# Another written order for the first two batches of an attention and expert kernel, with the loads placed anew

## The chip, the core and the metric

The kernel runs on one core of a Trainium2 chip. What counts is the time of one execution on the device in microseconds. Five engines work beside each other, each through its own list of instructions in order: TensorE (PE, with its weight loads as PEld), VectorE (DVE), ScalarE (ACT), GpSimd (POOL) and SyncE (SP), which here only issues the loads and stores. An instruction waits on semaphores for what it reads and for the buffer that it writes.

## What is computed

Attention in two steps with 32 packed queries, and then a layer of three products with a maximum:

```python
def sm_attn(qq, kk, vv):                       # head_dim 64
    s = scale * np.matmul(qq, kk.transpose(0, 1, 3, 2))
    s = s - np.max(s, axis=-1, keepdims=True)
    a = np.exp(s)
    a = a / (np.sum(a, axis=-1, keepdims=True) + 1e-09)
    return np.matmul(a, vv)
p_packed = sm_attn(p, k, v)                    # 8 batches, 8 heads, 32 x 64
out = sm_attn(q, p_packed, p_packed)           # 8 batches, 8 heads, 576 x 64
...
x = out.transpose(0, 2, 1, 3).reshape(4608, 512)
h = np.maximum(np.maximum(x @ w1, x @ w2), x @ w3)   # 512 -> 768
return (h @ w_out).astype(np.float32)                # 768 -> 512
```

All in float32.

## The kernel before

The work goes batch by batch, eight of them, 576 tokens each. Since `out` is a product of weights and `p_packed`, the kernel never forms x: it multiplies `p_packed` by the weights once (stage P, 4 x 2 blocks of 32 rows in 64 contraction rows) and the second softmax by that. Each product of N and O is formed from a high and a low part in the fp32r type, three matmuls for one.

The stages have letters. k, v, q and w are loads; w0 to w5 are the six column tiles of w1, w2, w3, each in three parts of 512 KB (`w01` is tile 0, part 1), and w6 is w_out. S is the scores of the packed queries with k (L226); A weighs them: DVE's maximum (L239) and scaling (L240), ACT's exp (L244), and, in the first two batches, the turning T of the weights by PE (L269, L270) and a copy. Z inverts the sums. V is the product with v (L312), K turns p_packed (L327) and copies it to `pt`. Q is the scores of q with it (L341), in two halves of 288 tokens. B (`attend`) is the second softmax: DVE's block transpose (L364), maximum (L368), subtraction (L370), ACT's exp (L372), sum (L375), reciprocal (L382), product (L384), transpose (L387) and the split into a2h and a2l (L126 to L131). C converts one part of a weight: two steps on ACT (L189, L194), one on DVE (L200), one on POOL (L204). P is p_packed @ w for one tile (L414), which ACT and DVE then split into ph (L425) and pl (L427). N (`layer_in`, L450) multiplies a2 by P, E takes the maximum (L465), H splits it, O (`layer_out`, L504) is the product with w_out, F scales and stores. P04 is batch 0, tile 4. The filler matmuls of `rouse` (L139, on the identity) are placed by a word `I10`: ten units of 128 columns ahead of the next product.

What sets the order: the words of the table START are taken one after the other, and each advances its stage by one step, so the table is the order of every engine's list for batches 0 and 1 and the first parts of batch 2. A letter v, g or a behind a word (`B000g`) names the engine of a step where there is a choice: DVE, POOL or ACT. Loads stand in the same table, and they go to SP's one queue in that order. Behind the table, a loop over batches 2 to 7 starts each batch's stages at the times of STAGES, counted in steps of PE, and only PE's order is fixed by hand there; for the batch 2 the loop begins with two tiles of P.

PSUM is two buffers of two banks (`ps_big`) for S, Q, the pairs of P and the T of batch 1, and four buffers of one bank (`ps_moe`) for N, O and the single tiles of P. So with S1 in both large buffers, the next product that wants one, P01, waits for the first exp of S1 (it is the last to read it), and the one behind, T10, for the second. Loads of k and v share four buffers, those of q two, of weights seven and four.

Where PE stands at a time is told by the word and its number: Q0's first half is at 14.47 us, its second at 18.81, P00 at 20.30, S1 at 25.73 and 27.10, P01 at 30.79, T10 at 31.60, V1 at 35.24, Q1 at 38.52.

Of the kernel before, what the change touches and what calls it, by code (L numbers as in the profile page):

```python
# [44 lines left out]


START = """
k01 k00 w00 I10 S0 A01 v00 v01 w02 C00 A01 A00 A00 I7 A01 A01v A00 q000 q010 C00 w01 I1 V01 C00 C00 A00v
Z00 Z01 q011 C02 V01 V00 q001 V00 w21 K0 K0v C02 C01 I1 Q0 C02 B000 B000 B010 C01 C02 B010 B000g C01
B000 B010v w11 w10 B000 w12 I8 Q0 B000a B010 C21 B001 B000 C21 C01 I3 P00 B011 B000g B001 B001g P00 B011  # L50
B000 C21 B011v B000a B000g C21 B001 B011 B010 B001 B010a B011 B010 k10 k11 C10 B001a w20 P00 I10 N00
B011a B001 B011 B001v B010v w32 w22 C10 C11 C10 I4 S1 B011v B010 B001 C12 C11 B010a C10 B011 B010v C11
C12 P00 C12 P00 B001a C20 N00 A10 N00 B011a v11 v10 C20 C11 A11 C12 A10 w40 A11 P01 B001v q10 q11 E000v
B011g E000 Z11 P01 C32 C32 C20 Z10 C20 A10 N00 N00 P01 C32 A10v A11 N00 C22 A11a E001v C40 C22 E000 V101
E001 V101 C32 N01 w30 w31 K1 C22 w61 E001 C22 C40 K1a H00a N01 w62 Q1 C30 E010v C40 H00v B11 B10 C40 C30
H00v N01 C30 C30 C31 N01 E010 B10 P02 P02 E010 C31 P10 B10g E011v w42 P02 N01 w63 C31 N01 B11 C61 w41
C31 E011 w60 B10 C42 E011 N02 C42 N02 P03 H01a N02 C42 N02 B10 E020v C42 B10v E020 H01g P03 C41 E021a
N02 N02 B11g E020 P03 C41 E021 H01v C41 N03 N03 C41 P10 B10 P10 E021 H02v E030v C61 B11 B11 E030 N03 w52
w51 w50 P11 P04 B10g C61 B11v C52 C62 E030 N03 C62 P04 C50 H02g N03 P04 B11 C63 H02a E031a B10 E031 N03
B10a N04 N04 E040a B11g C51 N04 E031 B11 E040 B10v C51 C51 B11a N04 B11v C50 C52 E041a N04 N04 H03a C61  # L60
E040 E041 E041 N10 H03v C62 C50 C52 H03a E100v H04a P11 N10 N10 C50 E100 C51 P11 E100 N10 C63 E101a N10
N10 N11 E101 H04v H04a E110v N11 N11 E110 C52 P05 P12 E101 N11 N11 P05 C61a H10a P05 E111a C60 P12 C62
E110 N11 C61g H10v E111 N05 E111 H11v P12 C60 C62a H10a E050a N05 N05 E050 N05 N12 E051v H11g E050 C62v
N05 N05 P13 P14 E051 N12 H11v E051 C60 E120a P14 H05v C63 N12 w64 w65 P13 H05g E120 C63 C60 N12 N12 N12
P13 E121a C65 E120 H05v N13 C63v E121 E121 E130a H12a q21 k20 k21 C64 C60a C65 P14 C64 N13 N13 C63g H12g
C60g E130 N13 P15 E131a E130 C64 P15 N13 N13 H12a C65 P15 E131 C64 N14 N14 S2 C64v E131 N14 N14 C65
E140v A20 O0 A21 C65v E140 E140 C65g C64v A20 A21 v21 q20 k30 X2 v20 X2 N14 O0 O0 O0 k31 E141v N14 O0 X2
O0 F00v E141 E141 Z21 O0 O0 O0 F01a O0 O0 F02a O0 N15 H13a F03v H13v H13a N15 N15 V201 E150v Z20 V201
N15 K2 N15 E150 N15 K2v E151v E150 E151 Q2 O1 O1 O1 B21 E151 H15a O1 B20 B21 H14a B20 H14v H15g O1 v31
O1 O1 B20v B21g B21 B20 O1 B20 P20 F10a B21 B21a v30 O1 O1 F11a B20a B20 B20g q31 B20 O1 H15v B21 q30  # L70
B21g B20a P20 B21 P20 B20g B21a O1 B21v F13a H14a F12v
"""

EXTRA = "12 05 13"
# [3 lines left out]
STAGES = "S1:2 k2:5 X1:7 P3:12 P4:12 P5:25 V1:25 K1:29 v2:28 Q1:36 P6:36 q2:38 P7:42 P8:42"  # L78
# [3 lines left out]
def fused_kernel(ctx: ExitStack, tc: tile.TileContext, kp, qt, va, vb, wi, wo, out):  # L82
# [483 lines left out]
    def begin(stage, at):  # L566
        due.append([at, len(due), stage])

    def tick():

        while True:
            ready = [d for d in due if d[2] is not None and d[0] <= clock[0]]
            if not ready:
                break
            d = min(ready, key=lambda d: d[:2])
            wait = next(d[2], None)
            while wait == 0:
# [14 lines left out]
    def issue(name, b, at):  # L592

        kind, n = name[0], int(name[1])
        if kind == "P":
            b, j = b + n // NJ, n % NJ
        else:
            b += n
        if b >= B:
            return  # L600
        if kind in loads:
            begin(both(loads[kind], b), at)
        elif kind == "P":
# [82 lines left out]
```

## Time and profile before

| | |
|---|---|
| median of three runs | 482.77 us (482.42 to 483.08) |
| profiled execution, its own time | 483.46 us |
| span of the profiled execution | 481.7 us |
| PE busy | 471.6 us (98% of the span) |
| DVE, ACT, POOL busy | 253.4, 191.2, 130.5 us |
| chain that ended last | PE 93%, DMA 5% |

The chain that ended last is the work followed back from the last instruction, at each step to what released it; it is PE's matmuls for 93% of the span. The span is cut into 40 slices of 12.04 us in the page, and a digit is the busy share in tenths.

### The profile page before, as it was taken

To read this page: it belongs to the slowest core of one execution; us is meant where nothing else is said; L and a number is where in the kernel's file an instruction comes from. 1 tells how busy PE (TensorE), PEld (TensorE's weight loads), DVE (VectorE), ACT (ScalarE), POOL (GpSimd) and SP (SyncE) were. 2 spreads that over 40 slices of the span, in tenths; PEclk is the share of its full clock that TensorE was granted. 3 is DMA by queue.
4 is the path that set the end of the run, shared out by engine and by line. 5 is a ranking of instruction groups with operands and counts; after the bars stand their busy time and mean duration, and the time that the engine had idled before them with its cause. 6 is when DMAs were issued, how large, how long until landed. Compare 5 with 4: busy or idle time off the path is not lost.

```text
span 481.7 us, 10570 instructions
## 1 busy us (share of the span) xinstructions
PE 471.6 (98%) x4352; PEld 388.6 (81%) x4352; DVE 253.4 (53%) x540; ACT 191.2 (40%) x409; POOL 130.5 (27%) x108
## 2 busy tenths in 40 slices
PE   7789999999999999999999999999999999999997
PEld 3367999888769987899679987899778987999885
DVE  2799988833656465444826455444816455244100
ACT  3687854401335334333424334333334334244211
POOL 0666754600322222022312223032212213144000
PEclk9999999999999999999999999999999999999999
DMA  8999221664245241423324242423221101100122
GB/s 298 398 378 405 97 81 72 216 177 148 69 169 144 60 151 49 156 44 99 105 84 138 51 136 79 152 51 101 98 88 25 27 2 45 44 1 1 44 67 65
DMA packets 36767, 55.60 MB, mean 115 GB/s; under 512 B 21488, under 2 KB 23792, under 8 KB 36720
## 3 DMA queue, kind: packets, MB, share of 16 engines
q1 hardware_dynamic: 36720, 54.93, 34.1%
q8 instruction: 34, 0.56, 0.5%
q14 instruction: 13, 0.11, 0.1%
HBM read 41.94 MB, written 9.44 MB: 107 GB/s over the span
## 4 chain that ended last, share of the span: by engine, by line
PE 93%; DMA 5%; ACT 0%; SPq 0%; issue 0%; DVE 0%; ACTq 0%
PE mi L450 48%; PE mo L504 32%; PE pw L414 7%; DMA wi<-in_wi 2%; PE av L312 2%; DMA q<-in_qt 2%; PE s L341 2%; DMA v<-in_va 2%; PE s L226 2%; PE tp L312 0%; PE tp L269 0%; SPq L160 0%; ACT wi L189 0%; PE av L327 0%; ACT a L244 0%
## 5 line engine op out<-in xcount | busy, mean ns | idle before, releaser
L450 PE MATMUL mi<-a2h,ph 128*128 128x288 f32 x576 | 173.6, 301 | 0.0
L450 PE MATMUL mi<-a2h,pl 128*128 128x288 f32 x576 | 169.8, 295 | 0.4 <-DVE pl L427 0.4
L450 PE MATMUL mi<-a2l,ph 128*128 128x288 f32 x576 | 169.7, 295 | 0.0
L465 DVE TENSOR_TENSOR hf<-mi,hf 128x288 f32<-128x288 f32 x192 | 86.5, 453 | 110.5 <-PE mi L450 87.5
L504 PE MATMUL mo<-h,wo_hi 128*128 128x512 f32 x432 | 139.5, 398 | 0.0
L450 PEld LDWEIGHTS mi<-a2h,ph 128*128 128x128 f32 x576 | 108.1, 188 | 13.5 <-issue 7.8
L450 PEld LDWEIGHTS mi<-a2h,pl 128*128 128x128 f32 x576 | 108.1, 188 | 1.0 <-DVE pl L427 0.7
L450 PEld LDWEIGHTS mi<-a2l,ph 128*128 128x128 f32 x576 | 108.1, 188 | 0.0
L131 POOL TENSOR_TENSOR h<-hf,h 128x512 fp32r<-128x512 f32 x36 | 46.5, 1292 | 220.0 <-ACT h L126 134.8
L504 PEld LDWEIGHTS mo<-h,wo_hi 128*128 128x128 f32 x432 | 81.0, 187 | 26.4 <-issue 4.2
L504 PE MATMUL mo<-h,wo_lo 128*128 128x512 f32 x216 | 85.3, 395 | 0.0
L427 DVE SCALAR_TENSOR_TENSOR pl<-pw,ph 128x768 fp32r<-128x768 f32 (+1 forms) x54 | 45.0, 860 | 34.7 <-ACT ph L425 34.5
L126 ACT COPY hf<-mi 128x288 f32<-128x288 f32 x83 | 33.0, 397 | 63.3 <-PE mi L450 58.2
L126 ACT CAST h<-hf 128x512 fp32r<-128x512 f32 x45 | 27.8, 620 | 60.4 <-DVE hf L465 60.4
L524 ACT ACTIVATE o<-mo 128x512 f32<-128x512 f32 x32 | 19.1, 597 | 77.7 <-PE mo L504 71.0
L504 PEld LDWEIGHTS mo<-h,wo_lo 128*128 128x128 f32 x216 | 40.5, 188 | 9.1
L425 ACT ACTIVATE ph<-pw 128x768 fp32r<-128x768 f32 (+1 forms) x54 | 37.9, 738 | 11.4 <-PE pw L414 10.8
L414 PE MATMUL pw<-w_sb,pt 64*32 64x384 f32 x768 | 38.2, 489 | 0.7 <-ACT a L244 0.7
L204 POOL TENSOR_TENSOR w_sb<-w_sb,wi 128x512 int32<-128x512 int32 x18 | 24.1, 1343 | 26.4 <-DVE w_sb L200 18.4
L370 POOL TENSOR_TENSOR e<-e,m 128x576 f32<-128x576 f32 (+1 forms) x15 | 16.7, 1127 | 29.8 <-DVE m L368 29.8
L131 POOL TENSOR_TENSOR a2l<-et,a2h 128x576 fp32r<-128x576 f32 (+1 forms) x13 | 17.5, 1348 | 21.0 <-ACT a2h L126 20.9
L414 PEld LDWEIGHTS pw<-w_sb,pt 64*32 64x32 f32 x768 | 11.4, 106 | 13.2 <-issue 11.4
(91 smaller groups left out, 339.4 us busy)
## 6 DMA issues: line engine op xcount, KB each, us to landing
kt<-in_kp SPq DMA_DIRECT2D x16, 640.0 KB, 5.2
wi<-in_wi SPq DMA_DIRECT2D x18, 512.0 KB, 8.2
out_t<-o SPq DMA_DIRECT2D x35, 256.0 KB, 2.0
v<-in_va SPq DMA_DIRECT2D x16, 512.0 KB, 4.6
q<-in_qt SPq DMA_DIRECT2D x14, 576.0 KB, 5.5
wo<-in_wo SPq DMA_DIRECT2D x6, 512.0 KB, 6.9
xt<-x SPq DMA_DIRECT2D x48, 40.0 KB, 2.0
xt<-x SPq DMA_DIRECT2D x48, 32.0 KB, 1.9
```

The lines of the kernel that those rows point to most:

```text
L126: e.copy(out=out, in_=src)
L131: on(default).tensor_tensor(out=lo, in0=src, in1=hi.bitcast(F32), op=ALU.subtract)
L204: nc.gpsimd.tensor_tensor(out=dst.bitcast(I32), in0=dst.bitcast(I32), in1=up, op=ALU.add)
L226: nc.tensor.matmul(out=s1[b][r][32 * n:32 * n + 32, hf, 0:HS], lhsT=kt[g][o, w:w + NP], rhs=kt[g][o, pr * S + hf * HS:pr * S + (hf + 1) * HS],
L370: on("g").tensor_tensor(out=e3, in0=e3, in1=m.unsqueeze(2).to_broadcast([P, nt, NP]), op=ALU.subtract)
L414: nc.tensor.matmul(out=ps[r][NP * n:NP * n + NP, 0:NW * P], lhsT=pt_sb[b % 2][o, NP * n:NP * n + NP], rhs=w_sb[o, j, n * NW * P:(n + 1) * ...
L425: nc.scalar.activation(out=hi[:, r], in_=x, func=AF.Copy, scale=2.0 ** -WS)
L427: nc.vector.scalar_tensor_tensor(out=lo[:, r], in0=x, scalar=2.0 ** -WS, in1=hi[:, r].bitcast(F32), op0=ALU.mult, op1=ALU.subtract,)
L450: nc.tensor.matmul(out=sums[b, j, hf, x][:, 0:HS], lhsT=w[:, r, x * P:(x + 1) * P], rhs=a[:, c], start=(r == 0 and n == 0), stop=(r == R - ...
L465: nc.vector.tensor_tensor(out=h, in0=sums[b, j, hf, i][:, 0:HS], in1=h, op=ALU.max)
L504: nc.tensor.matmul(out=sums[b, m], lhsT=w[:, j, m * P:(m + 1) * P], rhs=h[:, a], start=(j == 0 and i == 0), stop=(j == NJ - 1 and i == 2),)
L524: nc.scalar.activation(out=o, in_=ps, func=AF.Copy, scale=2.0 ** -WS)
```

## The change

The table START is written anew from end to end, with the same stages and steps, and the first tile of P of batch 2, `P1:0`, that the loop began with is now in it (as `P21`). Five single tiles and five pairs of P are in both. The fillers are 44 units before (10, 7, 1, 1, 8, 3, 10, 4) and 49 after (10, 7, 1, 1, 3, 27). A letter of choice differs at many words. The beginning of the table and the line of the loop:

```diff
-k01 k00 w00 I10 S0 A01 v00 v01 w02 C00 A01 A00 A00 I7 A01 A01v A00 q000 q010 C00 w01 I1 V01 C00 C00 A00v
+k01 k00 w02 v01 I10 S0 A01 C02 A01 v00 A00 Z01 A00 w12 I7 A01 A01v A00 A00v q000 C02 I1 V01 Z00 V01 C02
...
-            for x in (STAGES if b > 2 else "P1:0 P2:0 " + STAGES).split():
+            for x in (STAGES if b > 2 else "P2:0 " + STAGES).split():
```

On SP, the loads from the first weight behind v to k of batch 1 (kt2, kt3), before:

```order
L154 DMA wi0_2_119<-in_wi 128x512
L175 DMA q0_151<-in_qt 128x2x288
L175 DMA q1_153<-in_qt 128x2x288
L154 DMA wi0_1_156<-in_wi 128x512
L175 DMA q1_153<-in_qt 128x2x288
L175 DMA q0_151<-in_qt 128x2x288
L154 DMA wi2_1_218<-in_wi 128x512
L154 DMA wi1_1_249<-in_wi 128x512
L154 DMA wi1_0_251<-in_wi 128x512
L154 DMA wi1_2_255<-in_wi 128x512
L160 DMA kt2_315<-in_kp 128x1280
L160 DMA kt3_317<-in_kp 128x1280
```

and now:

```order
L154 DMA wi1_2_133<-in_wi 128x512
L175 DMA q0_157<-in_qt 128x2x288
L175 DMA q1_214<-in_qt 128x2x288 x2
L175 DMA q0_157<-in_qt 128x2x288
L154 DMA wi0_0_232<-in_wi 128x512
L154 DMA wi0_1_238<-in_wi 128x512
L154 DMA wi1_1_258<-in_wi 128x512
L154 DMA wi1_0_267<-in_wi 128x512
L160 DMA kt2_306<-in_kp 128x1280
L160 DMA kt3_308<-in_kp 128x1280
```

w00, which stood ahead of v, and w01 now come behind all four parts of q; w12 stands ahead of q, and w21 behind kt3. So the fourth part of q has one weight fewer in front of it, and kt3 too.

On PE, from N behind S1 to N behind T10 (S1 is s1_1, P01 is pw0_1), before:

```order
L450 MATMUL mi0_0_0_1_325<-a2h0_1_373,pl0_0_292 128x288
L450 MATMUL mi0_0_0_1_325<-a2l0_1_377,ph0_0_291 128x288
L450 MATMUL mi0_0_0_2_326<-a2h0_1_373,ph0_0_291 128x288
L450 MATMUL mi0_0_0_2_326<-a2h0_1_373,pl0_0_292 128x288
L450 MATMUL mi0_0_0_2_326<-a2l0_1_377,ph0_0_291 128x288
L414 MATMUL pw0_1_424<-w_sb_72,pt0_76 32x384 x8
L269 MATMUL tp1_0_455<-ident_67,a1_1_0_416 128x128 x4
L270 MATMUL tp1_0_455<-ident_67,a1_1_0_416 64x128
L450 MATMUL mi0_0_1_0_461<-a2h0_0_300,ph0_0_291 128x288
L450 MATMUL mi0_0_1_0_461<-a2h0_0_300,pl0_0_292 128x288
```

and now, from the end of S1:

```order
L226 MATMUL s1_1_0_334<-kt3_308 32x288
L226 MATMUL s1_1_1_335<-kt3_308 32x288
L450 MATMUL mi0_0_0_0_382<-a2h0_0_301,ph0_0_327 128x288
L450 MATMUL mi0_0_0_0_382<-a2h0_0_301,pl0_0_328 128x288
L450 MATMUL mi0_0_0_0_382<-a2l0_0_332,ph0_0_327 128x288
L450 MATMUL mi0_0_0_1_383<-a2h0_0_301,ph0_0_327 128x288
L450 MATMUL mi0_0_0_1_383<-a2h0_0_301,pl0_0_328 128x288
L450 MATMUL mi0_0_0_1_383<-a2l0_0_332,ph0_0_327 128x288
L414 MATMUL pw0_1_391<-w_sb_72,pt0_76 32x384 x8
L450 MATMUL mi0_0_0_2_384<-a2h0_0_301,ph0_0_327 128x288
L450 MATMUL mi0_0_0_2_384<-a2h0_0_301,pl0_0_328 128x288
L450 MATMUL mi0_0_0_2_384<-a2l0_0_332,ph0_0_327 128x288
```

Before, six N stood ahead of S1 and twelve between S1 and P01. Now P00 and S1 follow each other without N or filler, six N stand between S1 and P01, and N that stood ahead of P01 stand behind it.

On POOL, the conversions L204 and the steps of the second softmax of batch 0 between them, before:

```order
L204 TENSOR_TENSOR w_sb_72<-w_sb_72,wi0_1_156 128x512
L384 TENSOR_TENSOR e0_0_235<-e0_0_235,z2_0_0_0_253 128x288
L370 TENSOR_TENSOR e0_0_235<-e0_0_235,m2_0_0_288_288 128x288
L131 TENSOR_TENSOR a2l0_0_302<-et0_0_296,a2h0_0_300 128x288
L204 TENSOR_TENSOR w_sb_72<-w_sb_72,wi2_1_218 128x512
L204 TENSOR_TENSOR w_sb_72<-w_sb_72,wi1_0_251 128x512
L204 TENSOR_TENSOR w_sb_72<-w_sb_72,wi1_1_249 128x512
```

and now:

```order
L370 TENSOR_TENSOR e0_1_236<-e0_1_236,m2_0_1_0_253 128x288
L204 TENSOR_TENSOR w_sb_72<-w_sb_72,wi0_0_232 128x512
L384 TENSOR_TENSOR e0_0_228<-e0_0_228,z2_0_0_288_277 128x288
L204 TENSOR_TENSOR w_sb_72<-w_sb_72,wi0_1_238 128x512
L204 TENSOR_TENSOR w_sb_72<-w_sb_72,wi1_1_258 128x512
L204 TENSOR_TENSOR w_sb_72<-w_sb_72,wi1_0_267 128x512
L384 TENSOR_TENSOR e0_1_236<-e0_1_236,z2_0_1_288_295 128x288
```

w01 (wi0_1) stood first of these and now comes behind w00 and one L384; the L204 of w11 and w10 follow it directly.

On DVE, around the products L384 of that softmax, before:

```order
L382 RECIPROCAL z2_0_1_288_312<-z2_0_1_288_312 128x9
L384 TENSOR_TENSOR e0_0_235<-e0_0_235,z2_0_0_288_309 128x288
L384 TENSOR_TENSOR e0_1_239<-e0_1_239,z2_0_1_0_307 128x288
L200 TENSOR_SCALAR w_sb_72<-wi1_0_251 128x512
L384 TENSOR_TENSOR e0_1_239<-e0_1_239,z2_0_1_288_312 128x288
L387 STREAM_TRANSPOSE et0_1_368<-e0_1_239 128x288
L387 STREAM_TRANSPOSE et0_0_296<-e0_0_235 128x288
L387 STREAM_TRANSPOSE et0_1_368<-e0_1_239 128x288
L131 TENSOR_TENSOR a2l0_1_377<-et0_1_368,a2h0_1_373 128x288
```

and now:

```order
L382 RECIPROCAL z2_0_0_288_277<-z2_0_0_288_277 128x9
L384 TENSOR_TENSOR e0_0_228<-e0_0_228,z2_0_0_0_260 128x288
L370 TENSOR_TENSOR e0_1_236<-e0_1_236,m2_0_1_288_279 128x288
L200 TENSOR_SCALAR w_sb_72<-wi0_1_238 128x512
L382 RECIPROCAL z2_0_1_0_274<-z2_0_1_0_274 128x9
L384 TENSOR_TENSOR e0_1_236<-e0_1_236,z2_0_1_0_274 128x288
L375 TENSOR_REDUCE z2_0_1_288_295<-e0_1_236 128x9
L387 STREAM_TRANSPOSE et0_0_297<-e0_0_228 128x288
L387 STREAM_TRANSPOSE et0_1_303<-e0_1_236 128x288
L200 TENSOR_SCALAR w_sb_72<-wi1_0_267 128x512
```

The L200 of w01 now stands behind an L384 and an L370 and ahead of another L384; in the order before, w01's came far earlier, and w10's stands in this place.

## Rows read from the trace of the kernel before

**Rows 1.** The page's forty slices: PE's busy tenths and those of the transfers

```profile
PE   7789999999999999999999999999999999999997
...
DMA  8999221664245241423324242423221101100122
```

**Rows 2.** Windows: stretch, length, busy PE, PEld, DVE, ACT, POOL, clock, DMA share, GB/s

```profile
0.00:31.00 31.00, 24.47 (x257) 12.22 (x265) 19.37 (x56) 17.99 (x39) 13.53 (x18) 1.00 0.96 356
31.00:478.00 447.00, 447.00 (x4103) 376.43 (x4087) 233.61 (x483) 172.83 (x370) 116.92 (x91) 1.00 0.30 99
```

**Rows 3.** PE's waits for loads: engine, tile, releaser, total us, times, longest

```profile
PE s L341 <- DMA q<-in_qt: 1.6, 1, 1.6
PE s L226 <- DMA kt<-in_kp: 1.5, 2, 0.8
```

**Rows 4.** PE's timeline: start, duration, line, operation, count, and the idle time before

```profile
18.81 0.72 PE L341 MATMUL s<-q,pt 64*32 64x288 f32 x16 [1.61 <-DMA q<-in_qt]
...
20.30 0.88 PE L414 MATMUL pw<-w_sb,pt 64*32 64x384 f32 x16
21.11 2.42 PE L139 MATMUL mi<-ident 128*128 128x512 f32 x6
23.18 0.48 PE L450 MATMUL mi<-a2h,ph 128*128 128x288 f32 x1
...
27.10 1.18 PE L226 MATMUL s<-kt 64*32 64x288 f32 x24 [0.68 <-DMA kt<-in_kp]
...
28.45 0.29 PE L450 MATMUL mi<-a2h,pl 128*128 128x288 f32 x1
28.58 0.29 PE L450 MATMUL mi<-a2l,ph 128*128 128x288 f32 x1
...
30.79 0.88 PE L414 MATMUL pw<-w_sb,pt 64*32 64x384 f32 x16 [0.74 <-ACT a L244]
...
35.24 1.46 PE L312 MATMUL tp<-v,a1t 128*32 128x64 f32 x80
...
38.52 1.46 PE L341 MATMUL s<-q,pt 64*32 64x288 f32 x32
...
119.43 1.20 PE L341 MATMUL s<-q,pt 64*32 64x288 f32 x32
```

**Rows 5.** SP's timeline: issues that waited for earlier landings

```profile
21.40 0.33 SPq L166 DMA_DIRECT2D v<-in_va  x1
...
23.95 0.33 SPq L166 DMA_DIRECT2D v<-in_va  x1
```

**Rows 6.** Timelines of POOL, ACT and DVE: the conversions of w01 and w21

```profile
17.67 1.38 POOL L204 TENSOR_TENSOR w_sb<-w_sb,wi 128x512 int32<-128x512 int32 x1 [0.59 <-ACT e L372]
...
20.08 0.70 ACT L189 ACTIVATE wi<-wi 128x512 f32<-128x512 f32 x1 [1.23 <-DMA wi<-in_wi]
...
21.58 0.40 DVE L200 TENSOR_SCALAR w_sb<-wi 128x512 uint32<-128x512 uint32 x1
...
22.96 1.29 POOL L204 TENSOR_TENSOR w_sb<-w_sb,wi 128x512 int32<-128x512 int32 x1
```

**Rows 7.** DVE's timeline in batch 2: a subtraction beside POOL's

```profile
124.15 1.72 DVE L370 TENSOR_TENSOR e<-e,m 128x576 f32<-128x576 f32 x1
```

**Rows 8.** Groups by line: durations in ns, least, median and longest

```profile
L370 DVE TENSOR_TENSOR e<-e,m x3: 452/460/1717, 17.5 to 124.2; 128x288 f32<-128x288 f32 x2, 128x576 f32<-128x576 f32 x1
...
L204 POOL TENSOR_TENSOR wof<-wof,wo x6: 1308/1318/1757, 58.1 to 90.6; 128x512 int32<-128x512 int32 x6
```

**Rows 9.** Timelines of DVE and ACT: from S1's scaling to the next conversion

```profile
29.12 0.15 DVE L240 TENSOR_SCALAR nm<-mx 128x1 f32<-128x1 f32 x1
...
29.83 0.73 ACT L244 ACTIVATE a<-s,nm 128x576 f32<-128x576 f32 x1
...
31.77 0.81 ACT L425 ACTIVATE ph<-pw 128x768 fp32r<-128x768 f32 x1 [0.39 <-PE pw L414]
32.47 0.68 ACT L189 ACTIVATE wi<-wi 128x512 f32<-128x512 f32 x1
```

More of the change, by code (lines that the diff above doesn't have):

```diff
@@ L47 @@
 START = """
-k01 k00 w00 I10 S0 A01 v00 v01 w02 C00 A01 A00 A00 I7 A01 A01v A00 q000 q010 C00 w01 I1 V01 C00 C00 A00v
[L49 to L71, printed above, removed]
+k01 k00 w02 v01 I10 S0 A01 C02 A01 v00 A00 Z01 A00 w12 I7 A01 A01v A00 A00v q000 C02 I1 V01 Z00 V01 C02
+C12 V00 V00 C02 K0 C12 K0v q010 I1 Q0 C12 C12 B000 q011 q001 w00 B000 B010 w01 I3 Q0 B000g B000 C00 B010
@@ new lines @@
+B001 B001 w11 B000 B010g B010 C00 B001v B001 w10 B011 B000a C01 C00 C00 B010 B000 B001 B011 B001a B010a
+C01 B001 C11 B000v B011v C01 B001g B011 C10 B010 C10 B010v B011 B000 C11 C01 B000a B010 C10 k10 k11 I27
+P00 P00 B011a C11 B000v S1 w21 C11 B001 P00 A10 B011 w31 v10 B001a B010a C10 P00 B011g w22 v11 C21 A10
+N00 P01 B010g C21 w20 C31 P01 P00 A11 B011 N00 B011v C21 B001v A11 N00 A10 B011g C21 P01 A11 E000v C31
+q10 q11 E000 C31 C22 Z11 A11a C22 E000 N00 C20 N00 C31 C20 N00 A10v C22 w41 Z10 E001v C22 V101 N01 w32
@@ new lines @@
+E010a C41 w30 E001 V101 K1 C20 C41 C20 E001 K1v N01 H00v E010 Q1 N01 N01 H00g w61 C32 B11 B10 C41 B10
+E010 w42 P02 E011v H00a C32 P02 C41 C32 P10 C32 C30 C30 P02 N01 E011 N01 C30 N02 C30 N02 w62 w40 N02
+E020a E011 B11 H01a C42 P03 C42 N02 P03 E020 H01v B11v N02 E020 C42 N02 C42 B10g C40 P10 B11 C40 H01a
+P03 E021v N03 E030a P10 E021 C40 E021 w65 N03 w51 w60 C40 C51 C62 E030 N03 w50 H02a N03 B11 P04 q21 q20
+w52 B11v E030 B10 P04 C62 B10 B11 H02g B11g B10a P04 C61 P11 N03 B10 C62 C61 E031v N03 N04 C62 E031 B10g
@@ new lines @@
+E031 N04 B11 C50 P11 N04 H02a C62a C62v E040a B11a N04 B11g B10 E040 P12 C52 E040 B10a B10v H03a C52 C65
+N04 N04 C51 E041v C61 H03g C65 E041 N10 E041 C52 H03v C51 H04a N10 E100v H04g N10 N10 C61 N10 E101a C50
+E100 P11 E100 N10 C60 P12 E101 H04a N11 C65 E101 N11 N11 w64 E110a H10a P12 E110 N11 N11 E110 C51 C52
+C50 E111a C50 N11 E111 H10v N12 w63 P05 P13 N12 H10a C65 E120a E111 H11v P05 C60 N12 C63 H11g P05 E120
+C61v E120 C65a C61v N05 H11v N05 N05 E050v C65g N05 E050 E050 C60 P13 E051a C60 N12 N05 N12 E121v P13
@@ new lines @@
+E121 E051 N12 N05 E121 E051 N13 H05a P14 P15 C64 H12a N13 H05v H12v H05v N13 H12v N13 k20 P14 C60a E130a
+C63 N13 k21 P14 P15 E131a C64 E130 C60g N13 E130 E131 N14 C64 P15 E131 C63 C63 E140a C63a N14 C63g C64
+N14 v20 E140 N14 S2 k31 v21 A21 E140 O0 N14 k30 A20 E141a A20 E141 X2 A21 C64v X2 X2 O0 O0 C64v O0 N14
+O0 F00v O0 O0 F01a O0 N15 O0 O0 O0 E141 Z20 F02v Z21 O0 N15 H13v H13v N15 V201 H13a E150v E150 E150 F03v
+H14v v30 H14g V201 N15 N15 K2 E151v K2a N15 O1 Q2 E151 B20 E151 B21 H15a H15g B21 B21g O1 O1 O1 v31 B21
@@ L72 @@
+O1 B21 O1 B21v O1 q31 q30 B21 H14v B20 O1 O1 B20g F10a P21 B20 P20 O1 B21v B20 B21 B20v H15v O1 B20 B21a
+P20 B20g F12v B20 P21 F11a B20a B21g B20g O1 F13a P21 P20
 """
```

## The prediction

> **What bounds the kernel now.** I read the forty slices first, then a table of windows, then TensorE's waits, then the timelines of the stretch where it waits. The slices show PE at nine tenths from the fourth of forty on, 36 us, and the transfer engines at eight or nine for the first four, 48 us, and low after that [rows 1]. The windows say it sharply: PE is busy for 447.00 of the 447.00 us from 31 to 478, at a granted clock of 1.00, and for 24.47 of the first 31 [rows 2]. So the matmuls of 31 to 478 are a fixed sum, unless an order brings a wait into it, and a new order can win time only in the first 35 us. PE's waits for loads are 1.6 us for q and 1.5 for kt, in two parts [rows 3]. They and a wait for an exp lie in the ramp: 18.81 (Q0's second half waits 1.61 for q), 27.10 (the rest of S1 waits 0.68 for kt), 30.79 (P01 waits 0.74 for the exp of L244) [rows 4]. The windows hide a fourth: Q1 at 38.52 takes 1.46 us, and the same 32 matmuls take 1.20 at 119.43 [rows 4]. Its second half began with the landing of q3, so about 0.25 us of wait is counted as busy there. Beside these, filler matmuls (L139) stand in the ramp wherever PE would have stood still.
>
> What sets the ramp is the loads. Within it SP issues a load when an older one has landed; from the issue at 21.40 to the second one after it, at 23.95, it is 2.55 us, so 1.28 for each 512-KB weight load that landed in that time [rows 5]. So a load that moves past one weight load lands 1.28 us earlier or later.
>
> **The change part by part.** All useful matmuls stay: PE gets the same products, in another order, and 49 filler units in place of 44. The unit costs 0.207 us (ten units, 21.11 to 23.18, in [rows 4]). Five units more cost 1.0 us if they stood in the path; they don't by themselves, since 27 of the 49 now stand in one block ahead of P00, which waits for data anyway, as follows.
>
> (1) *Loads.* kt3 now has six weight loads ahead of it instead of seven, q3 ten instead of eleven, and the last quarter of the first q two instead of three. With 1.28 us each: Q0's second half can start at 18.81 - 1.28 = 17.53, S1's kt3 part at 27.10 - 1.28 = 25.82, and q3 lands about 37.5 in place of 38.8. The price is w01, which P00 needs with w00 and w02: it stood third among the weights, and its conversion on POOL ran from 17.67 to 19.05 [rows 6]. It now comes two weight loads behind the q, at 17.5 + 2 x 1.28 = 20.06.
>
> (2) *P00.* Before, it began at 20.30 without a wait [rows 4]. A load that landed at the same 20.06 is in the trace: w21, with ACT's L189 at 20.08, DVE's L200 at 21.58 (its end 21.98), POOL's L204 from 22.96 to 24.25, after 0.98 us in which POOL was in another step [rows 6]. Without that other step it would have ended at 21.98 + 1.29 = 23.3: the lower bound. In the changed order w00's L204 and an L384 of POOL stand in front of w01's, and on DVE an L384 and an L370 in front of its L200, so the 24.25 is the nearest. From above: DVE's and POOL's operations with two inputs in SBUF stretch where they meet. DVE's L370 at 124.15 takes 1.72 us [rows 7], beside POOL's L370, and two of its half-size form, 0.45 each, would be 0.9; POOL's L204 goes from a median of 1.32 to 1.76 [rows 8]. One such meeting costs 0.4 to 0.8 us, three cost 0.8 + 0.8 + 0.44, which puts the upper bound at 24.25 + 2.04 = 26.3. I take one hold-up of 0.75 on the nearest row: P00 at 25.0. The block of 27 fillers begins when Q0's second half is done, 17.53 + 0.65, and lasts 27 x 0.207 = 5.6 us, to 23.8; it is not late. Its cover is P00's own wait. Were w01 there at 23.3, the filler would cost 0.5.
>
> The Trainium skill ("SBUF — State Buffer", section "Who interferes with whom") says that a DVE instruction with two SBUF inputs contends with a GpSimd instruction that reads SBUF, and that the pair is locked for a whole instruction. By that rule each meeting would cost DVE up to one whole L204, 1.32 us by the row, and two of them would end P00's wait at 26.9 and make the sum +2.0, 484.8, where it is +0.1 by the rows; the 1.72 agrees in kind, the 1.38 of [rows 6] doesn't.
>
> (3) *S1.* It now follows P00 directly, where ten fillers, six N and four fillers lay between. Its first eight of 32 take 0.37 us, P00 takes 0.81 [20.30 to 21.11, rows 4], so its kt3 part starts at P00 + 1.18 or at 25.82, whichever is later: with P00 at 25.0, at 26.18, 0.92 earlier than the 27.10 of before. The point where the bound passes from kt3 to P00 is P00 = 24.64.
>
> (4) *From S1 to V1.* The six N that stood before S1 now stand behind it, and the next six move behind P01, so that the time won is taken up: before, from S1's kt3 part to V1 there were 30 N, now 36. P01 needs the PSUM buffer that the first exp of S1 frees. Before: kt3 part 27.10, DVE's maximum and its scaling done at 29.27, exp 29.83, P01 30.79 [rows 4, 9]; of this 0.56 us (29.27 to 29.83) the exp stood behind a conversion on ACT. In the new order w21's first conversion step (0.68 us) is ahead of the exp on ACT; it lands at 25.82 + 1.28 = 27.1 and is done at 27.8, before the scaling is (28.0). So P01 comes 2.17 (27.10 to 29.27) + 0.1 + 0.96 = 3.23 us after the kt3 part, and not 3.69. PE has 1.1 us of S1 and 1.0 of six N to do by then, and waits 1.1. Behind P01 the order of ACT puts P01's own ph in front of the second exp, which frees the buffer that T10 writes. From P01's start that is 0.98 to ph (30.79 to 31.77), 0.70 for it (to 32.47 [rows 9]), 0.96 from exp to release as above, so T10 at P01 + 2.64; PE's own work, P01 and 12 N, takes 2.5. Then T10 and T11 (0.52 and 0.46) and 18 N (18 x 0.133, from 28.45 to 28.58, and 0.18 for the switch): V1 at P01 + 6.19, where it was 35.24 - 30.79 = 4.45. In all V1 stands 9.42 us behind the kt3 part in place of 8.14. With that part at 25.82 it is 35.24, which is what it was; the 1.28 us gained in the landing are eaten, by N that now lie behind it and by the two exps. That PE has less to do ahead of S1 gives no time: it waits for P00 there.
>
> Which steps stand behind waiting instructions: on PE P01 holds N for 1.1 us, and on DVE the maximum of S1 waits for PE with w21's L200 queued behind it; w21 is needed for P02, which comes behind Q1 (38.52), some ten us later. POOL's three L204 in a row hold the second L384 and a2l of r=1, which the N after P01 read; w11's and w10's L204, 1.32 each behind w01's, are done near 28.2 (P01 needs w10 at 29.05), and the rest has until about 30.
>
> (5) *V1 to Q1.* The same steps on PE. Q1's second half finds q3 landed (37.5 against a Q1 at 38.5): 1.20 in place of 1.46, -0.25.
>
> (6) *The rest of the table.* P02 to P15, C, E, H, B and the loads of weights change places over 40 to 130 us, in which PE never waited [rows 2]. I read the margins from the times of before plus the shifts: P02 2.4 us, P03 0.7, P04 0.7 to 1.0 (w40 now lands near 46.7), the low halves of P03 to P05 0.35 to 0.5. The price is 0 as long as these hold; if one is missed, its overshoot, a few tenths; nothing can be gained there.
>
> (7) *P21.* Tile 1 of the third batch moves from the head of the loop, at 138.5, into the table a few us earlier. It costs PE the same in either place, about twice P00's 0.81 [rows 4], and its ACT and DVE steps lie beside PE's matmuls on engines that are busy for 39 and 52% of 31 to 478 [rows 2]. N2_0, which reads P20 first, has 18 products of O and P22 between; so 0.
>
> **The sum.** Against the profiled execution (483.46 us, 0.7 above the median of 482.77): P00's lateness 25.0 - 24.64 = +0.35, V1 0.0, Q1 -0.25. Together +0.1: a profiled execution of 483.6, and against the median 482.77 + 0.1 = 482.9. In general: change = (P00 - 24.64) - 0.25, for P00 over 24.64, and -0.25 under it.
>
> **The rivals.** A change of 0.2%, 0.97 us, is what a measurement of this kernel can tell from none: under 481.80 is faster, over 483.74 slower.
>
> *Slower: DVE and POOL hold each other up* in the conversion of w01, 22 to 26 us. P00 decides from 25.86 on: (25.86 - 24.64) - 0.25 = 0.97. The far end, P00 at 26.3, gives 484.2. For it: the row at 124.15 [rows 7], and a DVE order that now has L384, L370, L200, L384 in a row while POOL has L384 and three L204. Against it: at 17.67 in the kernel before POOL's L204 ran beside DVE's half-size L370 and lost 0.06, 1.38 for a median of 1.32 [rows 6, 8].
>
> *Slower or same: a weight is late.* P04 or a low half overshoots its margin, 0.3 to 0.8 us more, so 483.2 to 483.7 with the forecast's sum. By itself it hardly crosses 483.74; with P00 at 25.4 it does.
>
> *Faster: the landings move by more than 1.28 us* and P00 is at its lower bound of 23.3 to 23.9. Then S1 starts as soon as kt3 is there; each tenth that kt3 is earlier than 25.82 moves P01, V1 and Q1 with it until q3 (37.5, and it moves too). 0.7 us earlier gives -0.95, 481.8. The far end is P00 at its lower bound, 23.3, with the kt3 part at 24.48: 1.34 before 25.82, so -1.6, 481.2, with every landing 1.3 us early and the fillers early with them. Against it: the loads run at the rate of [rows 5] from the first us on, and the order alone doesn't make that faster.
>
> *The change does nothing:* the ramp ends on the same loads; with P00 under 24.64 it is -0.25, 482.5.
>
> **How the numbers follow.** The forecast with "nothing", P00 from 23.3 to 25.86, all margins held or missed by little: 0.70, all of it within 0.2%. P00 beyond 25.86: 0.14. A late weight on top that crosses 0.2%: 0.08. Faster: 0.08. The range reaches down to 481.9, which leaves out the faster case, and up to 484.2, the far end of P00, which leaves out about 0.1 above.
>
> **What would show it.** Right: P00 between 24.3 and 25.6 with a wait for POOL's L204, S1's kt3 part near 26, P01 with a wait for the exp of about 1.1 us, V1 within 0.5 us of 35.24, Q1 in 1.2 us, PE busy without a gap from 40 us on. Wrong: a wait for POOL or a pl behind 40 us (rival two), P00 over 25.86 with long L370 or L384 rows on DVE (rival one), kt3 landed before 25.2 (rival three).

## The result, and the profile after

The changed kernel takes 485.49 us (median of six, 484.32 to 486.18), beside 482.99 of the kernel before (six, 482.42 to 483.34); the ratio is 1.0048, with an interval of 1.0038 to 1.0059. It is slower, by 2.5 us as the difference of the medians and by 2.3 by the ratio. The forecast was no change, 482.9 in a range from 481.9 to 484.2.

| | before | after |
|---|---|---|
| profiled execution, its own time | 483.46 | 485.53 |
| span | 481.7 | 483.4 |
| time outside the span | 1.76 | 2.13 |
| first N behind Q1 on PE | 39.92 | 40.39 |
| S3 begins on PE | 141.76 | 143.69 |

The waits of PE in the new kernel (engine, line, what was waited for: us in total, times, longest):

```profile
PE s L139 <- POOL ident masks.py:199: 1.4, 1, 1.4
PE pw L414 <- ACT a L244: 1.2, 1, 1.2
PE pw L414 <- POOL w_sb L204: 0.8, 1, 0.8
PE mi L450 <- DVE pl L427: 0.8, 1, 0.8
PE pa L327 <- DVE pp L322: 0.4, 1, 0.4
...
PE s L226 <- DMA kt<-in_kp: 0.4, 1, 0.4
PE av L327 <- DVE pp L322: 0.3, 1, 0.3
```

The waits for q and kt that led this list before [rows 3] are gone or small (the 0.4 for kt is that of S0), and so is the wait of Q1. In their place stand P00's for POOL, N's for pl and a longer one of P01 for the exp. PE's timeline (start, duration, line, operation, count, idle before it):

```profile
15.93 0.72 PE L341 MATMUL s<-q,pt 64*32 64x288 f32 x16
...
22.57 0.84 PE L414 MATMUL pw<-w_sb,pt 64*32 64x384 f32 x4
24.20 0.54 PE L414 MATMUL pw<-w_sb,pt 64*32 64x384 f32 x6 [0.79 <-POOL w_sb L204]
...
24.62 1.75 PE L226 MATMUL s<-kt 64*32 64x288 f32 x30
...
27.47 0.40 PE L450 MATMUL mi<-a2h,pl 128*128 128x288 f32 x1 [0.78 <-DVE pl L427]
...
29.60 0.88 PE L414 MATMUL pw<-w_sb,pt 64*32 64x384 f32 x16 [1.20 <-ACT a L244]
...
35.91 1.53 PE L312 MATMUL tp<-v,a1t 128*32 128x64 f32 x80
...
39.26 1.20 PE L341 MATMUL s<-q,pt 64*32 64x288 f32 x32
...
120.27 0.33 PE L327 MATMUL av<-ident,pp 128*128 128x128 f32 x1 [0.32 <-DVE pp L322]
```

Against [rows 4]: Q0's second half comes 2.9 us earlier (15.93), S1's part on kt3, inside the row at 24.62, at 25.20, 1.9 earlier than 27.10, P01 1.2 earlier; and V1, 35.91, is 0.67 later than 35.24. Q1 takes 1.20, as forecast. So the loads did more than was claimed for them, and behind S1 more than all of it was lost. What the ramp costs against the profiled execution of before is 0.47 at the first N behind Q1. By 143 us PE is 1.9 late and by 150 us 1.7, and it stays so to the end. The last row, K2 waiting for pp, is one of the later places.

What the chain behind S1 ran into is on DVE (start, duration, line):

```profile
21.45 0.93 DVE L370 TENSOR_TENSOR e<-e,m 128x288 f32<-128x288 f32 x1
...
22.88 1.58 DVE L384 TENSOR_TENSOR e<-e,z 128x288 f32<-128x288 f32 x1
...
27.35 0.73 DVE L239 TENSOR_REDUCE mx<-s 128x1 f32<-128x576 f32 x1
28.12 0.15 DVE L240 TENSOR_SCALAR nm<-mx 128x1 f32<-128x1 f32 x1
```

and on POOL:

```profile
21.30 0.76 POOL L384 TENSOR_TENSOR e<-e,z 128x288 f32<-128x288 f32 x1 [0.19 <-DVE z L382]
22.85 1.29 POOL L204 TENSOR_TENSOR w_sb<-w_sb,wi 128x512 int32<-128x512 int32 x1 [0.79 <-ACT e L372]
```

DVE's product L384 at 22.88 takes 1.58 us, where DVE's three L384 of this size in the kernel before took 0.45 or 0.46; the L370 at 21.45, beside POOL's L384, takes 0.93. POOL's L204 beside the first takes 1.29, no more than others of its kind [rows 6]. It began 0.03 earlier than the L384. Both of DVE's steps end 0.32 behind the one on POOL. In the kernel before, where DVE's step began first, 0.22 ahead of POOL's L204 (1.38, [rows 6]), it kept its 0.45:

```profile
17.45 0.45 DVE L370 TENSOR_TENSOR e<-e,m 128x288 f32<-128x288 f32 x1
```

Behind the L384 stand the transposes, the L200 of w10 and w11, a2l and pl, then S1's maximum: PE finished S1 at 26.3, and the maximum began at 27.35. On ACT the exp comes 0.35 behind the scaling, behind w21's first step:

```profile
28.07 0.68 ACT L189 ACTIVATE wi<-wi 128x512 f32<-128x512 f32 x1
28.62 0.74 ACT L244 ACTIVATE a<-s,nm 128x576 f32<-128x576 f32 x1
```

The Trainium skill ("SBUF — State Buffer", section "Who interferes with whom") says that an instruction of DVE with two inputs in SBUF contends with one of POOL that reads SBUF, and that issue order decides who blocks. The trace agrees here: the L204, which was first, is not stretched, and the L384 ends 0.32 us behind it. It doesn't agree in batch 2 of the kernel before: POOL's L370 began first there, at 123.62, and both are longer, 1.63 us on POOL for its usual 1.16 and 1.72 on DVE [rows 7].

### The profile page after: what moved, and what is told of

Read it like the earlier page. It is cut to its first block, busy times and chain, and to the rows that moved or that the text cites. A ratio compares the mean times of both kernels' runs of the same rounds, so it can differ in the third digit from the quotient of the medians.

```text
span 483.4 us, 10569 instructions
## 1 busy us (share of the span) xinstructions
PE 473.9 (98%) x4354; PEld 389.5 (81%) x4354; DVE 253.2 (52%) x540; ACT 190.2 (39%) x407; POOL 132.5 (27%) x110
## 4 chain that ended last, share of the span: by engine, by line
PE 84%; DMA 7%; DVE 4%; ACT 2%; SPq 1%; issue 1%; POOL 1%; DVEq 0%; ACTq 0%
PE mi L450 44%; PE mo L504 28%; PE pw L414 7%; DMA wi<-in_wi 3%; DMA kt<-in_kp 2%; PE av L312 1%; DMA v<-in_va 1%; PE s L341 1%; PE s L226 1%; SPq L292 1%; DVE hf L465 1%; POOL wof L204 1%; DMA out_t<-o 0%; DVE e L384 0%; DVE w_sb L200 0%
## 5 line engine op out<-in xcount | busy, mean ns | idle before, releaser
L131 POOL TENSOR_TENSOR h<-hf,h 128x512 fp32r<-128x512 f32 x37 | 47.9, 1294 | 213.8 <-ACT h L126 111.5
L204 POOL TENSOR_TENSOR w_sb<-w_sb,wi 128x512 int32<-128x512 int32 x18 | 24.0, 1338 | 26.1 <-DVE w_sb L200 13.4
L131 POOL TENSOR_TENSOR a2l<-et,a2h 128x576 fp32r<-128x576 f32 (+1 forms) x15 | 20.3, 1354 | 23.1 <-ACT a2h L126 22.8
L370 POOL TENSOR_TENSOR e<-e,m 128x576 f32<-128x576 f32 (+1 forms) x15 | 16.7, 1126 | 32.6 <-DVE m L368 32.5
```

Of the source, the lines that this page charges most:

```text
L131: on(default).tensor_tensor(out=lo, in0=src, in1=hi.bitcast(F32), op=ALU.subtract)
L204: nc.gpsimd.tensor_tensor(out=dst.bitcast(I32), in0=dst.bitcast(I32), in1=up, op=ALU.add)
L370: on("g").tensor_tensor(out=e3, in0=e3, in1=m.unsqueeze(2).to_broadcast([P, nt, NP]), op=ALU.subtract)
```

## The experiments

For a wider base I first read the same stretch in all traces. Up to Q1, four kernels share the table of before and five that of after. The first N behind Q1 is at 39.92, 39.11, 39.35 and 38.86 in the old ones (before, and three below), on average 39.31, and at 40.39, 40.38, 40.25, 40.45 and 40.48 in the new, on average 40.39. The new ramp costs 1.1 us, not 0.5: the profiled execution of before was the slowest of its four, since its loads landed later (Q0's second half, which waits for q, is at 18.81 there and at 18.02 to 18.47 in the others). These are single executions, and the four old ones lie 1.06 apart, so the 1.1 has a few tenths of doubt. PE's rows of the kernel "p21_alone" below, whose table is that of before to this point:

```profile
18.02 0.72 PE L341 MATMUL s<-q,pt 64*32 64x288 f32 x16 [1.06 <-DMA q<-in_qt]
...
26.32 1.17 PE L226 MATMUL s<-kt 64*32 64x288 f32 x24 [0.71 <-DMA kt<-in_kp]
...
34.45 1.46 PE L312 MATMUL tp<-v,a1t 128*32 128x64 f32 x80
...
37.73 1.20 PE L341 MATMUL s<-q,pt 64*32 64x288 f32 x32
```

Q0's second half is 0.8 earlier than in [rows 4], S1's kt3 part and V1 too, and Q1 takes 1.20: the 0.25 that the forecast gave the change there was no loss of the old kernel but of that one execution.

**Two halves of the tables, cut at Q1 and at S2.** The words of one table up to the cut, then those of the other that are still to come, in their order.

> The table of after up to the word that issues Q1 (about 39 us), and the order of before for all that is left; P21 stays in the loop. Theory A (the new ramp costs only what PE shows at Q1, and later waits make the rest): V1 near 35.9 and +0.5 to +0.9 us against before, 483.5 to 483.9. Rival B (the whole loss is made in the ramp by DVE and POOL holding each other up, what comes later follows from it): as slow as after, 485.0 and more.

> The table of before up to the word that issues Q1, and the order of after for all that is left, with P21 in the table. Theory A: the waits of after at 53 us (0.4), at 115.7 (0.2) and at K2 (0.5) are there or most of them, 484.0 to 484.8. Rival B: no loss, 482.8 to 483.2.

490.95 (490.77 to 492.15, ratio 1.0171, 1.0158 to 1.0184) and 487.98 (487.13 to 488.27, 1.0101, 1.0088 to 1.0114). Neither theory: the seam makes waits of its own. A tile of P waits in both, for a weight in the first and for DVE in the second:

```profile
47.23 1.39 PE L414 MATMUL pw<-w_sb,pt 64*32 64x384 f32 x16 [5.01 <-POOL w_sb L204]
```

```profile
43.75 1.52 PE L414 MATMUL pw<-w_sb,pt 64*32 64x384 f32 x32 [2.79 <-DVE e L364]
```

The order in which weights are loaded and the order in which they are converted belong together, and the cut parts them. The two say nothing on the question, apart from their ramps.

> The table of after up to S2 (94 us), where all of w1 to w3 is converted in both tables, and the order of before behind it, P21 in the loop. Theory A (three places: the ramp, ACT's wait for w40 near 50 us, DVE's wait for a store near 105 to 115 us): the ramp's 0.3 to 0.5 us on PE and in some executions w40's 0.4, no wait of K2; 483.4 to 484.2. Rival B (all of it made in the ramp): as after, 485.2 and more.

> The table of before up to S2 and the order of after behind it, with P21 in the table. Theory A: K2 waits 0.3 to 0.5 us for pp behind the finish that waits for its store, 0.2 more at 115; 483.4 to 483.9. Rival B: as before, 482.9. If P21's place costs something it shows here too, behind 130 us.

The first is 488.39 (486.88 to 488.58, ratio 1.0107, 1.0092 to 1.0122), with a seam again: its O0 waits for DVE's maxima, which stand in another order:

```profile
PE mo L504 <- DVE hf L465: 2.3, 1, 2.3
```

The second is 483.02 (482.46 to 483.37, eleven runs; ratio 1.0000, 0.9991 to 1.0009), as the kernel before. So the new order behind S2 costs nothing when the old one stands ahead of it. That agrees neither with my 483.4 to 483.9 nor with a loss at K2 that belongs to the tail alone.

**One letter of the finish.**

```diff
-O0 F00v O0 O0 F01a O0 N15 O0 O0 O0 E141 Z20 F02v Z21 O0 N15 ...
+O0 F00v O0 O0 F01a O0 N15 O0 O0 O0 E141 Z20 F02a Z21 O0 N15 ...
```

> After, with one letter changed: the third finish of batch 0 goes to ACT instead of DVE, so that DVE does not stand for 9.2 us on the buffer that the first store has to free behind the 16 xt transfers on SP. Theory A: no excess at 115.7 and no wait of K2 for pp, 0.7 us off after: 484.8. Rival B: the same as after, 485.5.

484.69 (484.19 to 485.66, five runs; ratio 1.0037, 1.0025 to 1.0049). That is 0.8 less than after, but 0.35 if the executions at the lower clock (below) are left out on both sides. In the kernel after DVE stands at this place (start, duration, and the idle time before):

```profile
114.97 0.69 DVE L526 TENSOR_SCALAR o<-mo 128x512 f32<-128x512 f32 x1 [9.22 <-DMA out_t<-o]
...
118.81 0.68 DVE L526 TENSOR_SCALAR o<-mo 128x512 f32<-128x512 f32 x1
...
119.74 0.47 DVE L322 TENSOR_SCALAR pp<-av,r 128x64 f32<-128x64 f32 x2
```

and SP issues in front of the store whose buffer it waits for:

```profile
100.69 11.84 SPq L292 DMA_DIRECT2D xt<-x  x16
112.63 7.23 SPq L528 DMA_DIRECT2D out_t<-o  x4
```

The third finish writes the buffer of the first, whose store stands on SP behind sixteen transfers xt. DVE stands still for 9.2 us and comes late to its next steps: among them a cast, two maxima, the fourth finish at 118.81 and another cast, and only then pp at 119.74, for which K2 waits. With the finish on ACT:

```profile
116.41 0.68 DVE L526 TENSOR_SCALAR o<-mo 128x512 f32<-128x512 f32 x1
...
117.48 0.48 DVE L322 TENSOR_SCALAR pp<-av,r 128x64 f32<-128x64 f32 x2
```

```profile
119.01 0.27 PE L327 MATMUL av<-ident,pp 128*128 128x128 f32 x1
```

pp comes 1.07 behind the fourth finish here too, but that one is 2.4 us earlier, and K2 doesn't wait. In the five traces with the new ramp and `F02v` the excess in front of K2 is 0.35 to 0.48 us; in the three with `F02a` it is none, and in the one with `F02v` behind the old order (s2_old_new, where DVE waits 7.27 and not 9.2) none either. In h2_ramp_old, which has the old ramp and the new order from Q1 on, the excess is there, 0.39, with a wait of DVE of 8.91:

```profile
122.14 0.33 PE L327 MATMUL av<-ident,pp 128*128 128x128 f32 x1 [0.24 <-DVE pp L322]
```

So this is a loss of about 0.5, of the letter together with the new order between Q1 and S2, and not of the ramp. In the profiled execution of after 0.2 more is lost at 115.7 us; that too is gone with the letter, but fill4 and rampfix don't have it either.

**The wait for w40.**

```diff
-C42 B10g C40 P10 B11 C40 H01a
+C42 B10g P10 B11 C40 C40 H01a
```

> After, with the first conversion step of w40 on ACT moved behind P10's ph and the exp of e1_1, so that ACT does not wait for w40's landing (50.10) ahead of them. Theory A: the excess of 0.4 at 52.98 goes, 485.1; if w40's landing is what differs between executions, the spread of after (484.3 to 486.2) shrinks too. Rival B: the same as after, 485.5.

485.02 (484.61 to 486.15, six runs; ratio 1.0047, 1.0034 to 1.0060). The excess at 53 us is gone, but it is not in other traces with the old place either. ACT in the kernel after, and in "fill4", which has the same order here:

```profile
50.18 0.68 ACT L189 ACTIVATE wi<-wi 128x512 f32<-128x512 f32 x1 [0.60 <-DMA wi<-in_wi]
```

```profile
49.48 0.68 ACT L189 ACTIVATE wi<-wi 128x512 f32<-128x512 f32 x1
```

ACT took w40 without a wait in the five other traces with this order (f02a, s2_new_old, rampfix, fill4, i15): it had landed at 47.2 to 48.6 in four of them, and at 49.7 in i15, where all of this comes later. In that one execution it landed at 50.10. The 0.4 us are that execution's. The spread is not from here: it is 1.5 us, where it is 1.9 in the kernel after.

**The stretched product moved.** DVE's L384 goes behind the sum and the transpose that followed it.

```diff
-C10 B010v B011 B000 C11 C01 B000a B010
+C10 B011 B000 C11 C01 B000a B010v B010
```

> After, with one product L384 of DVE (the one that took 1.58 us at 22.88 beside POOL's L204) moved behind the sum and the transpose that followed it, so that these do not stand behind its stretch. If the meeting of DVE and POOL is what makes the ramp late: N's wait for pl at 27.47 shrinks by 0.5 us, the exp comes at 28.1 and V1 near 35.4 instead of 35.9, 485.0. If not: V1 near 35.9, 485.5.

484.16 (483.51 to 484.82, eight runs; ratio 1.0025, 1.0015 to 1.0035), 1.3 less than after. DVE's and PE's rows:

```profile
23.36 0.47 DVE L387 STREAM_TRANSPOSE et<-e 128x288 f32<-128x288 f32 x1
23.76 0.81 DVE L384 TENSOR_TENSOR e<-e,z 128x288 f32<-128x288 f32 x1
...
26.85 0.75 DVE L239 TENSOR_REDUCE mx<-s 128x1 f32<-128x576 f32 x1
```

```profile
26.98 0.40 PE L450 MATMUL mi<-a2h,pl 128*128 128x288 f32 x1 [0.16 <-DVE pl L427]
...
29.09 0.88 PE L414 MATMUL pw<-w_sb,pt 64*32 64x384 f32 x16 [1.19 <-ACT a L244]
...
35.41 1.46 PE L312 MATMUL tp<-v,a1t 128*32 128x64 f32 x80
```

The L384 now meets only the end of POOL's L204 (22.95 to 24.25) and takes 0.81, again to 0.32 behind it. The maximum begins 0.5 earlier, N's wait for pl falls from 0.78 to 0.16, P01 is at 29.09, V1 at 35.41: 0.5 of the 1.3 us, as expected. The rest I put to the next point.

**The lower clock.** Every execution has a mean granted clock. In the kernels with the new ramp as it was (after, f02a, c40_later) five of 17 executions show 0.996 and take 485.7 to 486.2, some 1.2 more; the others show 0.998 to 1.000 and have medians of 484.6 to 484.9. In the kernel before none of 74 does. In rampfix and the two kernels with three edits, 27 executions, none does. But it is not the new ramp's alone: s2_new_old and h2_ramp_old, which wait behind their seams, show 0.995 or 0.996 in three of four each, and before_plus (below), which has the old order nearly throughout, in one of eleven, at 484.97, again about 1.1 over its others.

```diff
-P00 A10 ... A10 N00 P01
+P00 A10 ... A10 I4 N00 P01
```

> After with four filler units (0.83 us) ahead of the first N of batch 0, where PE waits 0.78 us for pl. Nothing else moves. If the executions of after whose mean granted clock is 0.996 and which take 1.2 us more get it from PE's idle time between 22 and 30 us: none of them here, and a median near 484.9. If the filler stands in the path, or the clock falls elsewhere: 485.5 or more, with a third of the executions at 0.996.

484.78 (484.32 to 485.30, five runs; ratio 1.0041, 1.0028 to 1.0053), none of the five at 0.996; V1 at 35.98, as after. The fillers cost nothing, and five runs are too few by themselves. So the other way, with less filler in the block before P00:

```diff
-C01 B000a B010 C10 k10 k11 I27
+C01 B000a B010 C10 k10 k11 I15
```

> After with 15 filler units ahead of P00 instead of 27, so that PE stands idle for about 2.5 us more before 22.5, and does the same useful work. If the clock falls where PE has long waits between 20 and 30 us: most executions below 0.998, a trace with a granted clock under 1.00 in a stretch behind P00, and 1 to 3 us more than after in those. If the lower clock has its place elsewhere: 485.5 and a third of the executions at 0.996, as after.

486.99 (485.48 to 487.32, four runs; ratio 1.0072, 1.0056 to 1.0088); the four show 0.988, 0.989, 0.989 and 0.995. The trace has the place (stretch; busy us and count of PE, PEld, DVE, ACT, POOL; granted clock; DMA share; GB/s):

```profile
core 0: us, PE busy (x) PEld busy (x) DVE busy (x) ACT busy (x) POOL busy (x), PEclk, DMA share, GB/s
...
20.00:22.00 2.00, 0.79 (x5) 0.14 (x4) 1.52 (x6) 1.96 (x8) 1.71 (x2) 1.00 1.02 412
22.00:24.00 2.00, 0.28 (x2) 0.00 (x0) 1.97 (x4) 1.78 (x4) 1.21 (x2) 0.86 1.00 403
24.00:26.00 2.00, 1.52 (x24) 1.12 (x32) 2.00 (x5) 1.25 (x3) 0.42 (x1) 0.50 1.04 414
...
30.00:32.00 2.00, 1.95 (x18) 0.74 (x19) 1.93 (x6) 1.36 (x3) 1.51 (x2) 0.50 1.05 357
32.00:34.00 2.00, 2.00 (x11) 2.00 (x11) 1.72 (x4) 2.00 (x5) 1.54 (x2) 0.58 1.01 391
34.00:36.00 2.00, 2.00 (x19) 2.00 (x18) 1.97 (x7) 0.89 (x3) 1.09 (x1) 1.00 1.01 353
```

PE is busy for 0.79 and 0.28 us in two stretches of 2 us, and at 23.4 the granted clock falls to 0.50, that is 1.2 GHz of 2.4. It stays there to 33.7 us, through S1, N and P01, which are useful work (the 0.86 and 0.58 are stretches with both levels). V1 is at 37.76, 1.85 later than in after. So the clock can fall in this ramp, and more waiting makes it fall. No trace has caught one of the 0.996 executions of after, so that their dip lies there too is inferred from i15, fill4 and rampfix, not seen. It can lie elsewhere: in the trace of h1_ramp_new, at a mean of 0.995, the clock is down from 47.5 to 50.9 us, behind the wait of 5.01:

```profile
48.00:50.00 2.00, 2.00 (x25) 0.49 (x10) 1.74 (x4) 1.33 (x2) 2.00 (x2) 0.50 0.89 352
```

**All three edits, and P21.**

> After with three edits at once: the third finish of batch 0 on ACT, w40's first conversion step behind P10's ph and the exp, and the L384 moved as above. Theory A: no wait of PE behind 40 us and V1 near 35.4: the span like that of before, 483.0 to 483.6. If something else costs time (a lower granted clock in some executions, time outside the span), what is left over 483 shows it.

> The kernel with the three edits, and P21 moved back from the table to the head of the loop. If P21's place is what adds 0.35 us outside of the span: the time minus the span is 1.8 instead of 2.1, and 483.5. If not: 483.87 as with the three edits alone.

> Before with P21 alone moved into the table, behind P20, as a pair on PE. The forecast's step (7) priced it at 0: 482.9 to 483.1 and a time minus span of 1.8. If it is P21 that adds outside of the span: 2.1, 483.3.

483.87 (483.52 to 484.03, eleven runs; 1.0018, 1.0009 to 1.0027), 484.18 with P21 back in the loop (483.89 to 484.42, eight; 1.0025, 1.0015 to 1.0035), and 482.54 for P21 alone in the kernel before (482.20 to 483.14, eleven; 0.9993, 0.9984 to 1.0001). The three edits take away 1.6 of the 2.5 us and PE has no wait behind 40 us. P21's place, which I had put at 0, is worth 0.2 by S3's rows (the medians differ by 0.3 with the three edits and by 0.5 in the kernel before, where the interval of the ratio takes in 1). S3 in the kernel before, and with P21 alone moved:

```profile
141.76 1.67 PE L226 MATMUL s<-kt 64*32 64x288 f32 x32
```

```profile
140.71 1.45 PE L226 MATMUL s<-kt 64*32 64x288 f32 x32
```

S3 writes both large PSUM buffers, and in the old order P21 and P22 stand together ahead of it, with twelve N between; that it waits a little for each to be read is how I take these rows. The eleven kernels with P21 in the table have 1.45 or 1.46 here, the five with it in the loop 1.67 or 1.68.

The time outside of the span is 2.07 to 2.19 in all executions of the eight kernels that have the table of after throughout, but for single edits, and 1.73 to 1.90 in the kernels of which the table's end is that of before; P21 doesn't change it (2.12 with it back). With the end of after behind the head of before it varies from 1.75 to 2.12. That is 0.33 of the 2.5, and no row shows what it is.

**Two of the gains in the kernel before.** w40 behind q2 and q3 and its first two conversion steps behind Q1; w20's second step behind the exps of S1:

```diff
-v11 v10 C20 C11 A11 C12 A10 w40 A11 P01 B001v q10 q11 E000v
+v11 v10 C11 A11 C12 A10 A11 C20 P01 B001v q10 q11 w40 E000v
...
-E001 C22 C40 K1a H00a N01 w62 Q1 C30 E010v C40
+E001 C22 K1a H00a N01 w62 Q1 C40 C40 C30 E010v C40
```

> Before with two of the things that the change got right, and no other: the load of w40 behind those of q2 and q3 (its first two conversion steps behind Q1 accordingly), and the second conversion step of w20 behind the two exps of S1 on ACT. By the chain of the forecast: exp 0.5 earlier, P01 0.5 earlier, V1 earlier by as much unless the load of v holds it, Q1 0.25 shorter: 482.2 to 482.7. If the loads of v (landing near 34.8) hold V1: 482.6 to 482.9.

> Before with P21 in the table behind P20 (alone: 482.54, 0.2 us off S3), and w20's second conversion step on ACT behind the two exps of S1, with no load moved. If both add up: P01 0.35 us earlier, V1 too, 482.2, faster than before by 0.8 and than after by 3. If DVE's queue or the load of v takes the 0.35 back: 482.5.

483.81 (483.27 to 484.97, eleven runs; 1.0020, 1.0011 to 1.0029). The exp did come 0.4 earlier and V1 with it (34.45, with Q0's second half at 18.37 where the old order has 34.45 for 18.02), but P02 then waited 0.55. The conversion of w40 stood on DVE ahead of the transposes that free P02's buffer, which I take for the cause; the profile names POOL's L204, which ended at the same time, and no run parts the two. Without the load moved and with P21 in the table: 482.81 (481.95 to 483.38, eleven; 0.9993, 0.9984 to 1.0001). V1 is as early, at 34.42, but Q1 takes 1.82, because q3 lands at 38.30. So no version is clearly faster than the kernel before; P21 alone is the nearest.

## Why the prediction was wrong, point by point

**What bounds.** Right in that the middle can only lose: PE was busy for 446.5 of the 447 us from 31 to 478. Wrong in what the profiled execution stood for. The forecast saw that it was 0.7 over the median and added its change to the median all the same; but the terms were taken from its rows. 0.6 of the 1.1 us that the new ramp costs was hidden there.

**(1) Loads.** Right in direction, too small: kt3 landed so that its part began at 25.20 (forecast 25.82), Q0's second half began at 15.93 (17.53), P00's last weight was converted at 24.14. In the four traces with the old ramp the kt3 part begins at 26.69 on average, so the loads gained 1.5 against a usual execution, where 1.28 was forecast. kt3 landed at 25.15, which was set as a sign of the faster rival (before 25.2), and the kernel is slower all the same.

**(2) P00.** It was the term on which the sum was built, 0.35 for a hold-up of POOL. P00 began at 22.57 and went on at 24.20; POOL was not held. The formula with P00 as its one variable gave -0.25.

**(4) S1 to V1.** The step that failed. From the kt3 part to P01 it is 29.60 - 25.20 = 4.40 in place of 3.23; from P01 to V1 6.31 for 6.19. So V1 stands 10.71 behind the kt3 part, and not 9.42; in the old order it is 8.14. With the 1.5 of the loads that is the ramp's loss: 10.71 - 8.14 - 1.5 = 1.1, where 9.42 - 8.14 - 1.28 = 0 was forecast. The 2.17 from S1's part to the end of the scaling were copied from the old order, in which DVE came free just as S1 ended (28.27 and 28.28). They measured 3.07: in the new order PE reached S1 earlier and DVE was late, behind an L384 that took 1.1 us too long. With that L384 at 0.81, in rampfix, it is 2.47. ACT's exp came 0.35 behind the scaling, where 0.1 was forecast, since ACT's casts ahead of w21's conversion had waited 0.85 for DVE's transposes, and the conversion began at 28.07 though w21 landed at 26.4. The slower rival had the mechanism, and looked for it in P00 and on POOL, where the chain had slack; it hit DVE, which had none.

**(5) Q1.** 1.20 as said; but no gain against a usual execution of before.

**(6) The rest.** The margins that were read held (w40's landing, forecast at 46.7, made ACT wait in one trace alone). The loss came at a step that was not on the list: K2, behind a finish that waits for a store behind xt on SP. About 0.5.

**(7) P21.** 0 forecast, about 0.2 gained.

**Not thought of:** a lower granted clock in five of 17 executions, by an estimate 0.35 to 0.55 us (five of 17 by about 1.2 is 0.35; the median of after without its two is 484.94 in place of 485.49), and 0.33 outside of the span.

Summed: 1.1 for the ramp, 0.5 for K2, 0.35 to 0.55 for the clock, 0.33 outside, -0.2 for P21: 2.1 to 2.3 of 2.3 to 2.5. The terms come from single traces and from medians, so the fit is in part luck. What remains, at most 0.4, is within the spread of single executions and was not traced. So the step that failed, (4), explains the ramp's 1.1, less than half of the miss; the rest are terms that the forecast had at 0 or did not have.

## What to carry to other kernels

Where a new order makes one engine reach a point earlier, the steps behind it are to be timed on the queues of the engines that it hands over to, not copied from the old order, in which those engines came free in time. A step with two operands in SBUF on DVE that began just behind one of POOL's ended only 0.32 us behind it, here 1.1 us late for a step of 0.45; so it belongs where nothing urgent stands behind it on DVE, or ahead of POOL's. And a single profiled execution is to be placed among its runs by the step that made it slow before its rows are used as terms.

## What the runs showed that was not expected

In i15 the granted clock fell to 0.50 for about 10 us in the middle of a ramp, behind two stretches of 2 us in which PE was busy for 0.79 and 0.28, and the useful matmuls behind it paid: the twelve fillers that i15 lacks pay for themselves, though they only stand in front of a wait. With the 27 units of after and 2.8 us of waits in seven (0.79, 0.78 and 1.20), it seems to happen in some executions only.
